# First sweep of a fused attention and feed-forward kernel: six held feed-forward units for each mixing step, and the last tokens' sums a slot later

## The chip, the core and the metric

The kernel runs on one core of one Trainium2 chip. The metric is device time in microseconds (us) of one execution. The engines are TensorE (PE, its weight loads PEld), VectorE (DVE), ScalarE (ACT), GpSimd (POOL) and SyncE (SP, which issues most transfers). Matrix results land in PSUM banks, from which VectorE and ScalarE fetch them. A bank can be written anew only when it has been fetched.

## The reference

```python
# B, H, S, D = 8, 8, 576, 64; d_model 512, rank 32, hidden 2048
scores = (1/sqrt(D)) * q @ k.T
cum = cumsum(log(clip(f, 1e-4, 1)))
scores = where(causal, -1e9, scores + cum[:, None] - cum[None, :])
attn = exp(scores - max(scores)); attn = attn / (sum(attn) + 1e-9)
x = (attn @ v), heads side by side            # (8, 576, 512)
u = x + ((x^T @ U) @ V)^T                     # mixing along the tokens, rank 32
out = u + relu(u @ w_ch1) @ w_ch2             # feed-forward
```

All in float32. The kernel splits each operand in a high and a low half and multiplies high by high, low by high and high by low, so one float32 product is three passes.

## The kernel before

The work is in two sweeps. The second (from about 740 us) does ten of the sixteen hidden chunks of the feed-forward part for all tokens and is not touched. The first does attention for 32 head pairs, four to a batch, and, beside it, the mixing and six of the sixteen hidden chunks.

**Steps and slots.** The function `step(t)` works on head pair t, and finishes pairs t-1 and t-2. A step has ten slots. In each slot TensorE gets, in this order: one score block (`score`, `score_tail`; lines L357, L358), transposes of the exponentials of the pair before (L453, in slots 0 to 2 and 6 to 8; of the last tokens, L467, in slot 5), in slots 0 and 7 a product with the values (L556), and in slots 3, 4 and 8 the turn of the result (L587), the small turn (L486, L488) and the projection on the rank (L622). After these comes what was left over for the step: a mixing unit, and a feed-forward unit (a filler). TensorE's order and the transfers' (SP) are as written; VectorE, ScalarE and GpSimd are ordered by a scheduler when the program is built. What follows a matmul on other engines is written into a list by `defer(phase, fn, slots)`, which hands it out that many slots later, lower phases first.

**Mixing steps.** When four pairs of batch b are done, the next step (t = 6, 10, 14, ..., 30) carries its ten mixing units, one to a slot: H0 to H4 in slots 0 to 4 (`hmix`, matmul L650, whose result VectorE adds to X at L651), Tu0 to Tu3 in slots 5 to 8 (`tu`, four transposes L664; ScalarE copies the high half, uh, L654; VectorE makes the low half, ul, L655), Tv in slot 9 (`tv`, L673).

**Feed-forward units.** Of each batch there are two groups of tokens. A unit A (`l1`, L713) is one hidden chunk; ScalarE takes the relu (hh, L721) and VectorE the low half (hl, L717). A unit B (`l2`, L731) is one of three parts of the output sum for 128 tokens; x names the block of tokens, and p0, p1, p2 the parts, which stay in one bank until the third is done. Then `use` adds X on VectorE (ost, L745) and SP stores it. For odd batches the second group has a third block, of the last 64 tokens of two batches (ci = 4); its `use` is the two adds L748 and L749. This block comes first of its group's B units.

**Banks.** H, Tu, Tv, A and B take banks of one pool, psF (tag F), which has two. Scores have two of their own (psS). A score's bank is free again when VectorE has taken its maximum (L378, L404) and ScalarE its exponential (L386, L414).

**What sets the order.** In a mixing step a held unit runs after the mixing unit in four slots:

```python
HELD = 4
...
if filler and (s in (0, 1, 3, 5) or ending):
    run_filler()
elif len(filler) > HELD and s in ROOM:
```

In the three steps between, the other units are spread over eight slots each (ROOM, all but 0 and 7) by a running credit, so that HELD remain. The held ones are the last B units of the batch: x0p2, x1p0, x1p1, x1p2. At the end of the sweep what is held goes beside the mixing of the last batch, where the second sweep's weights are decoded as well (`wb_unit`, VectorE lines L70 to L87).

Of the kernel before, what the change touches and what calls it, by code (L numbers as in the profile page):

```python
# [13 lines left out]
ALU = mybir.AluOpType  # L14
# [9 lines left out]
NM = 4  # L24
# [11 lines left out]
NX = 3  # L36
# [4 lines left out]
def tile_decay_attention_moe(ctx, tc, qk, v, f, U, V, w1, w2, out):  # L41
    nc = tc.nc
# [10 lines left out]
    def behind(ins, kind):  # L53
        tc.add_manual_dep(
            ins.ins, newest[kind].ins.name,
            mybir.DependencyInfo(mybir.DependencyClass.NoSync, mybir.DependencyReason.DATA), reason=f"order behind {kind}",
        )
# [80 lines left out]
    xn = [cst.tile([P, NM + 1, DM], F32, name=f"xn{i}") for i in range(NX)]  # L138
# [122 lines left out]
    filler = []  # L261
# [4 lines left out]
    def defer(phase, fn, slots=1):  # L266
        later.setdefault(now[0] + slots, []).append((phase, fn))
# [6 lines left out]
    def run_filler():  # L274
        w, fn = filler.pop(0)
        fn()
        return w
# [417 lines left out]
    def ffn_units(b):  # L695
        X = xn[b % NX]
        groups = ((0, 256), (256, 256)) if b % 2 == 0 else ((0, 256), (256, 384))
        units = []
        for t0, nt in groups:
            g = {}  # L700

            def l1(fc, t0=t0, nt=nt, g=g):
                uh, ul = cur
                if fc == 0:
                    g["hh"] = sf.tile([P, NA, 384], F32R, tag="hh", name=f"hh{b}_{t0}")
                    g["hl"] = sf.tile([P, NA, 384], F32R, tag="hl", name=f"hl{b}_{t0}")
                hh, hl = g["hh"], g["hl"]
                sl = slice(t0, t0 + nt)
                ps = psF.tile([P, 512], F32, tag="F", name=f"A{b}_{t0}_{fc}")
                m = 0  # L710
                for c in range(NDC):
                    for wt, ut in ((w1h, uh), (w1l, uh), (w1h, ul)):
                        nc.tensor.matmul(ps[:, :nt], wt[:, fc, c], ut[:, c, sl], start=m == 0, stop=m == 3 * NDC - 1)  # L713
                        m += 1

                def low():
                    nc.vector.scalar_tensor_tensor(  # L717
                        hl[:, fc, :nt], ps[:, :nt], 0.0, hh.bitcast(F32)[:, fc, :nt], op0=ALU.max, op1=ALU.subtract
                    )

                defer(3, lambda: nc.scalar.activation(hh[:, fc, :nt], ps[:, :nt], AF.Relu))  # L721
                defer(1, low, 2)

            def l2(x, part, t0=t0, g=g):
                hh, hl = g["hh"], g["hl"]
                if part == 0:
                    g["ps"] = psF.tile([P, 512], F32, tag="F", name=f"B{b}_{t0}_{x}")
                ps = g["ps"]
                for fc in range(2 * part, 2 * part + 2):
                    for m, (ht, wt) in enumerate(((hh, w2h), (hl, w2h), (hh, w2l))):  # L730
                        nc.tensor.matmul(  # L731
                            ps, ht[:, fc, P * x : P * x + P], wt[:, fc],
                            start=fc == 0 and m == 0, stop=fc == NA - 1 and m == 2,
                        )
                if part < NA // 2 - 1:
                    return
                ci = t0 // P + x

                def use():
                    if b == B - 1 and ci < NM:  # L740
                        nc.vector.tensor_tensor(X[:, ci], ps, X[:, ci], op=ALU.add)
                        return
                    ost = sf2.tile([P, DM], F32, tag="ost", name=f"ost{b}_{ci}")
                    if ci < NM:
                        nc.vector.tensor_tensor(ost, ps, X[:, ci], op=ALU.add)  # L745
                        nc.sync.dma_start(accd[b, ci], ost)
                    else:
                        nc.vector.tensor_tensor(ost[0:64], ps[0:64], X[0:64, NM], op=ALU.add)  # L748
                        nc.vector.tensor_tensor(ost[64:128], ps[64:128], xn[(b - 1) % NX][0:64, NM], op=ALU.add)  # L749
                        nc.sync.dma_start(accd[B, b // 2], ost)  # L750

                defer(1, use)

            units += [(12 * max(nt / 2400, 0.107), lambda fc=fc, l1=l1: l1(fc)) for fc in range(NA)]
            units += [
                (6 * 0.216, lambda x=x, part=part, l2=l2: l2(x, part)) for x in ((2, 0, 1) if nt > 2 * P else (0, 1)) for part in range(NA // 2)
            ]
        return units
# [1 line left out]
    NP = B * NHP  # L760
    SLOTS = 10
    ENGINES = (nc.scalar, nc.scalar, nc.gpsimd, nc.gpsimd, nc.gpsimd)
    HELD = 4
    with tc.manual_schedule(engines=None):
        fr, fl, cm0, dq = decay_log()
        nc.sync.dma_start(fr, f)
# [41 lines left out]
    def step(t):  # L808
# [3 lines left out]
        last, ending = t == LAST, t > LAST - 2  # L812
# [7 lines left out]
        for s in range(6 + 2 if last else SLOTS):  # L820
# [71 lines left out]
            if mixing:  # L892
                for _ in range(2 if t == MIX[0] else 1):
                    mixing.pop(0)[1]()
                if filler and (s in (0, 1, 3, 5) or ending):
                    run_filler()
            elif len(filler) > HELD and s in ROOM:

                ahead = sum(x >= s for x in ROOM) + len(ROOM) * (min(m for m in MIX if m > t) - 1 - t)
                credit[0] += (len(filler) - HELD) / max(ahead, 1)  # L900
                if credit[0] > 0.999 or t > LAST - 3:
                    credit[0] = max(credit[0] - 1, 0)
                    run_filler()
            if ps_ and s == 6:
                score(p, 1, 0)
            if px and s == (6 + 1 if last else 9) and st[c]["hp"] == NHP - 1:
                b = st[c]["b"]
                assert len(filler) <= HELD and not mixing
                mixing.extend(mix_units(b))
# [9 lines left out]
    with tc.manual_schedule(engines={ET.PE, ET.SP}):  # L919
        step(0)  # L920
    with tc.manual_schedule(engines={ET.PE}):
        for t in range(1, 7):
            step(t)
    with tc.manual_schedule(engines={ET.PE, ET.SP}):
        for t in range(7, LAST + 1):
            step(t)
        run_later()
# [585 lines left out]
```

## Time and profile before

| | |
|---|---|
| median of 3 runs | 1218.68 us (1218.43 to 1220.3) |
| the profiled execution | 1220.24 us |
| its span, first to last instruction | 1218.4 us |
| TensorE's granted clock | 1.000 |
| mixing step 10 (score of slot 0 to the next step's) | 181.06 to 201.79 |
| step 15 | 292.05 to 313.62 |

All durations below are of the profiled execution. A row in order of time has its start (us from the span's start), its length, engine, line, operation, tiles written and read (buffer numbers left out), sizes, count, and in brackets the idle time before it and what ended that. Matmuls overlap: the next can start before the modelled end of the last, so the distance between two starts tells more than the length. S is a score, St one of the last tokens, P and Ptl exponentials, T and T_v their transposes, PTh and PTl the two halves fetched from these, G the operands of the next scores, xh and xl the halves of the attention output.

### The profile page before, as it was taken

The numbers are of one execution on the slowest core, as the hardware profiler recorded it, in microseconds if no ns is written. First come the engines' busy times: TensorE is split into PE (matmuls) and PEld (weight loads), VectorE is DVE, ScalarE is ACT, GpSimd is POOL, SyncE is SP. The second block draws the span as 40 slices with busy tenths as digits, with TensorE's granted clock in tenths as the row PEclk, the third lists the DMA queues.
The fourth block names the chain that finished last, engine by engine and source line by source line (L and its number), as shares of the span: only waits on it lengthen the run. The fifth ranks groups of instructions, "written<-read, shape, count | busy, mean of one in ns | idle before, by whom it ended". The sixth has DMA issues, their size and how long they took to land.

```text
span 1218.4 us, 23835 instructions
## 1 busy us (share of the span) xinstructions
PE 1187.9 (97%) x8460; PEld 1084.7 (89%) x8460; DVE 931.2 (76%) x2249; ACT 738.6 (61%) x2027; POOL 523.9 (43%) x518
## 2 busy tenths in 40 slices
PE   8998999999999999999999999999999999999998
PEld 5887898988889988989989887788999999999998
DVE  8887878768778778787686798966777767778675
ACT  7777787767768758777676443434454544545443
POOL 4214554544545535454442000024575556555553
PEclk9999999999999999999999999999999999999999
DMA  5753335325235325425322357132514244243420
GB/s 155 194 140 122 102 87 167 102 78 168 75 88 167 90 79 150 119 70 177 81 85 83 110 175 216 54 104 70 156 53 139 89 137 123 91 134 92 134 53 36
DMA packets 81159, 138.47 MB, mean 114 GB/s; under 512 B 8752, under 2 KB 45616, under 8 KB 78992
## 3 DMA queue, kind: packets, MB, share of 16 engines
q1 hardware_dynamic: 79824, 128.56, 35.1%
q0 software_dynamic: 1152, 8.39, 3.7%
q8 instruction: 67, 1.10, 0.4%
q14 instruction: 52, 0.43, 0.1%
q10 hardware_dynamic: 64, 0.00, 0.0%
HBM read 101.08 MB, written 35.78 MB: 112 GB/s over the span
## 4 chain that ended last, share of the span: by engine, by line
PE 79%; DVE 10%; ACT 6%; issue 2%; DMA 2%; POOL 0%; SPq 0%; DVEq 0%; ACTq 0%; POOLq 0%
PE N L1156 12%; PE A L713 10%; PE A L1136 9%; PE B L731 9%; PE B L1136 7%; PE V L556 5%; PE T L453 4%; PE V L528 3%; PE S L357 3%; PE S L358 2%; PE B L1156 2%; PE S L354 2%; DMA sr<-in_w_dram 2%; PE O L1027 2%; PE O L1221 1%
## 5 line engine op out<-in xcount | busy, mean ns | idle before, releaser
L386 ACT ACTIVATE P<-S,nm 128x128 f32<-128x128 f32 (+3 forms) x256 | 137.5, 538 | 54.3 <-DVE nm L378 47.4
L197 POOL TENSOR_TENSOR hb<-xn,hb 128x256 fp32r<-128x256 f32 x136 | 113.6, 856 | 125.7 <-ACT hb L194 104.4
L378 DVE CUSTOM_DVE_ANT_0 S<-S,mask 128x128 f32<-128x128 f32 (+3 forms) x256 | 125.6, 496 | 53.4 <-PE S L358 46.5
L322 POOL CAST G<-qk 64x576 fp32r<-64x576 f32 x52 | 34.7, 667 | 248.9 <-PE St L358 148.2
L713 PE MATMUL A<-uh,w1h 128*128 128x256 f32 (+1 forms) x384 | 120.6, 314 | 1.9 <-DVE hl L717 1.9
L713 PE MATMUL A<-ul,w1h 128*128 128x256 f32 (+1 forms) x384 | 113.7, 296 | 0.0
L713 PE MATMUL A<-uh,w1l 128*128 128x256 f32 (+1 forms) x384 | 113.6, 296 | 0.0
L194 ACT CAST hb<-xn 128x256 fp32r<-128x256 f32 x136 | 51.8, 404 | 77.4 <-DVE xn L1142 42.9
L731 PE MATMUL B<-w2h,hh 128*128 128x512 f32 x216 | 90.5, 419 | 1.7 <-DVE ost L745 1.0
L453 PE MATMUL T<-ident,P 128*128 128x128 f32 x544 | 85.5, 273 | 0.0
L731 PE MATMUL B<-w2l,hh 128*128 128x512 f32 x216 | 85.1, 394 | 0.0
L731 PE MATMUL B<-w2h,hl 128*128 128x512 f32 x216 | 84.7, 392 | 0.0
L435 DVE TENSOR_TENSOR PTl<-T,PTh 128x512 fp32r<-128x512 f32 (+1 forms) x156 | 79.0, 524 | 6.6 <-ACT PTh L432 6.3
L1156 PE MATMUL N<-sw,hb 128*128 128x256 f32 x546 | 80.4, 283 | 0.1
L335 POOL TENSOR_TENSOR G<-qk,G 64x576 fp32r<-64x576 f32 x52 | 74.4, 1432 | 13.1 <-PE T L453 5.1
L1156 PE MATMUL N<-b2h,hb 128*128 128x256 f32 x420 | 79.9, 282 | 0.0
L336 POOL TENSOR_TENSOR G<-qk,G 64x576 fp32r<-64x576 f32 x52 | 75.3, 1449 | 4.9 <-ACT G L322 4.6
L713 PEld LDWEIGHTS A<-uh,w1h 128*128 128x128 f32 x384 | 72.9, 190 | 4.3 <-DVE hl L717 4.1
L357 PE MATMUL S<-G 128*128 128x128 f32 x208 | 70.3, 343 | 4.8 <-ACT P L386 3.1
L432 ACT CAST PTh<-T 128x512 fp32r<-128x512 f32 (+1 forms) x156 | 68.3, 469 | 10.1 <-PE T L453 9.6
L713 PEld LDWEIGHTS A<-uh,w1l 128*128 128x128 f32 x384 | 73.2, 191 | 0.3
L713 PEld LDWEIGHTS A<-ul,w1h 128*128 128x128 f32 x384 | 72.9, 190 | 0.0
(328 smaller groups left out, 3999.1 us busy)
## 6 DMA issues: line engine op xcount, KB each, us to landing
qk<-in_qk_dram SPq DMA_DIRECT2D x104, 288.0 KB
direct<-ud SPq DMA_DIRECT2D x48, 256.0 KB
sr<-in_w_dram SPq DMA_DIRECT2D x20, 512.0 KB
vr<-in_v_dram SPq DMA_DIRECT2D x32, 256.0 KB
accd<-ost SPq DMA_DIRECT2D x32, 256.0 KB
xn<-accd SPq DMA_DIRECT2D x8, 1024.0 KB
out_dram<-xn SPq DMA_DIRECT2D x32, 256.0 KB
ud<-uh SPq DMA_DIRECT2D x7, 1024.0 KB
```

The source lines that it names most:

```text
L197: leng.tensor_tensor(dl, src, dh.bitcast(F32), op=ALU.subtract)
L335: pin(el.tensor_tensor(g[oth, 2, cols], k[oth], gf[oth, 2, cols], op=ALU.subtract))
L336: pin(em.tensor_tensor(g[own, 1, cols], q[own], gf[own, 0, cols], op=ALU.subtract))
L357: nc.tensor.matmul(ps, G[j][:, 0, c0 : c0 + P], G[j][:, 2, cols], start=first, stop=False)
L378: newest["top"] = nc.vector.tensor_tensor_reduce(ps[:, :w], ps[:, :w], mask[:, 512 - w : 512], scale=-SCALE, scalar=3.0e38, op0=ALU.add, o ...
L386: nc.scalar.activation(pt, ps[:, :w], AF.Exp, bias=z["nm"][:, col : col + 1], scale=-1.0, accum_out=z["sm"][:, col : col + 1])
L435: defer(2, lambda: nc.vector.tensor_tensor(dstl, src, dsth.bitcast(F32), op=ALU.subtract))
L453: nc.tensor.transpose(tp[:, P * x : P * x + P], z["P"][j][i][:, P * c : P * c + P], ident)
L713: nc.tensor.matmul(ps[:, :nt], wt[:, fc, c], ut[:, c, sl], start=m == 0, stop=m == 3 * NDC - 1)
L731: nc.tensor.matmul(ps, ht[:, fc, P * x : P * x + P], wt[:, fc], start=fc == 0 and m == 0, stop=fc == NA - 1 and m == 2,)
L1136: nc.tensor.matmul(ps, a[x][:, c], b[y][:, c], start=start and m == 0, stop=m == 5, skip_group_check=not start)
L1156: nc.tensor.matmul(ps[:, y], a[p_][:, P * y : P * y + P], w[q_], start=start and y == 0 and m == 0, stop=stop and y == 1 and m == 2,)
```

## The change

Six units are held for a mixing step instead of four (x0p0, x0p1, x0p2, x1p0, x1p1, x1p2), and run in slots 0, 1, 2, 4, 5 and 7. The three steps between have two units fewer, so their units stand in other slots. The last tokens' adds are handed out two slots after their third part instead of one, and are put behind the newest maximum in VectorE's order (`behind`: a mark for the scheduler, no wait).

```diff
                     else:
-                        nc.vector.tensor_tensor(ost[0:64], ps[0:64], X[0:64, NM], op=ALU.add)
-                        nc.vector.tensor_tensor(ost[64:128], ps[64:128], xn[(b - 1) % NX][0:64, NM], op=ALU.add)
+                        behind(nc.vector.tensor_tensor(ost[0:64], ps[0:64], X[0:64, NM], op=ALU.add), "top")
+                        behind(nc.vector.tensor_tensor(ost[64:128], ps[64:128], xn[(b - 1) % NX][0:64, NM], op=ALU.add), "top")
                         nc.sync.dma_start(accd[B, b // 2], ost)
 
-                defer(1, use)
+                defer(1, use, 1 if ci < NM else 2)
...
-    HELD = 4
+    HELD = 6
...
-                if filler and (s in (0, 1, 3, 5) or ending):
+                if filler and (s in (0, 1, 2, 4, 5, 7) or ending):
```

Three places in the built order. First ScalarE in mixing step 10, slots 4 to 6 (L492 the small turn, L322 the next pair's operands, L606 xh, L654 the high half of Tu). Before:

```order
L492 CAST PT49_2385<-Ty9_8_2482 64x128
L322 CAST G0_91<-qk11_0_2364 128x576 x2
L432 CAST PTh9_2383<-T9_v_2435 128x2x2x64 x2
L606 CAST xh8_2492<-xn2_106 128x640
L654 CAST uh0_1310<-Tu1_0_2506 128x4x128
L414 ACTIVATE Ptl10_2523,sm10_2354<-St10_0_2477,nm10_2353 128x288
L414 ACTIVATE Ptl10_2523,sm10_2354<-St10_1_2497,nm10_2353 128x288
L432 CAST PTh9_2383<-T9_10_2537 128x512
L654 CAST uh0_1310<-Tu1_1_2542 128x4x128
```

and the same piece of ScalarE's order with the change:

```order
L492 CAST PT49_2371<-Ty9_8_2469 64x128
L606 CAST xh8_2486<-xn2_106 128x640
L322 CAST G0_91<-qk11_0_2350 128x576 x2
L432 CAST PTh9_2369<-T9_v_2419 128x2x2x64 x2
L414 ACTIVATE Ptl10_2514,sm10_2339<-St10_0_2464,nm10_2338 128x288
L414 ACTIVATE Ptl10_2514,sm10_2339<-St10_1_2491,nm10_2338 128x288
L654 CAST uh0_1310<-Tu1_0_2500 128x4x128
L432 CAST PTh9_2369<-T9_10_2528 128x512
L654 CAST uh0_1310<-Tu1_1_2533 128x4x128
```

The copy of Tu0 (L654, Tu1_0: batch 1, block 0) moved behind the two exponentials of the last tokens, and xh moved ahead of the operands.

Second, VectorE in the same step, slots 3 to 5, with the change (L589 the turned result, L504 the last rows of it, L496 the small turn's low half):

```order
L435 TENSOR_TENSOR PTl9_2370<-T9_v_2419,PTh9_2369 128x128
L745 TENSOR_TENSOR ost0_2_2434<-B0_256_0_2379,xn0_104 128x512
L378 ISA S10_03_2445,nm10_2338<-S10_03_2445,mask_93 128x512
L378 ISA nm10_2338 128x1
L589 TENSOR_TENSOR xn2_106<-Tx8_2448,rv8_2317 128x4x128
L651 TENSOR_TENSOR xn1_105<-H1_3_2453,xn1_105 128x512
L404 ISA St10_0_2464,nm10_2338<-St10_0_2464,mask_93 128x288
L404 ISA nm10_2338 128x1
L651 TENSOR_TENSOR xn1_105<-H1_4_2472,xn1_105 64x512
L496 TENSOR_TENSOR PT49_2371<-Ty9_8_2469,PT49_2371 64x128
L504 TENSOR_TENSOR xn2_106<-Ty9_8_2469,rv8_2317 64x128
```

Before, the row of L745 for this bank stood two slots earlier, and the rest in the same order; now the sum of block x0 stands at the head of this piece.

Third, VectorE around the last tokens' adds of batch 1. Before, in step 13, slot 7:

```order
L435 TENSOR_TENSOR PTl12_3279<-T12_10_3439,PTh12_3278 128x512
L748 TENSOR_TENSOR ost1_4_3455<-B1_256_2_3391,xn1_105 64x512
L749 TENSOR_TENSOR ost1_4_3455<-B1_256_2_3391,xn0_104 64x512
L378 ISA S13_10_3450,nm13_3246<-S13_10_3450,mask_93 128x128
L378 ISA nm13_3246 128x1
L378 ISA S13_11_3463,nm13_3246<-S13_11_3463,mask_93 128x256
```

and with the change, in mixing step 14, slot 1:

```order
L378 ISA S14_00_3536,nm14_3522<-S14_00_3536,mask_93 128x128
L378 ISA nm14_3522 128x1
L748 TENSOR_TENSOR ost1_4_3571<-B1_256_2_3431,xn1_105 64x512
L749 TENSOR_TENSOR ost1_4_3571<-B1_256_2_3431,xn0_104 64x512
L427 TENSOR_SCALAR sm13_3232<-sm13_3232 128x9
L428 RECIPROCAL rv13_3816<-sm13_3232 128x9
```

The adds moved from ahead of a maximum in step 13 to behind the first maximum of step 14.

On TensorE the units between mixing steps change slots. Slots 5 and 6 are where the prediction looks. Before, one of the two is empty in steps 15, 17, 23 and 25, and in 28, whose slot 6 holds an A unit of 384 tokens instead of 256. With the change one is empty in steps 7, 8, 11, 12, 13, 17, 20, 21, 25, 28 and 29; in 8, 12, 20 and 28 slot 6 is the empty one and slots 4 and 5 hold B units. At the end of the sweep two B units move from between the last small transposes and the last rank product to behind the first mixing units of batch 7.

## The prediction

> **What bounds the kernel now.** I began with the page's busy times, then took the waits of TensorE, then the first sweep by stretches of one step each, then single waits in order of time.
>
> ```profile
> PE 1187.9 (97%) x8460; PEld 1084.7 (89%) x8460; DVE 931.2 (76%) x2249; ACT 738.6 (61%) x2027; POOL 523.9 (43%) x518
> ```
>
> TensorE is the bound, and its matrix work does not change here. What the change can move is only the time in which TensorE waits. The table of waits (engine and line, waited for: us in total, times, longest) names the feed-forward banks:
>
> ```profile
> PE Tu L664 <- DVE ost L745: 2.1, 6, 0.3
> PE Tu L664 <- DVE ul L655: 1.0, 1, 1.0
> ```
>
> Six times means once in each mixing step that holds feed-forward units (steps 10, 14, 18, 22, 26, 30). A row of this table counts only idle time after the modelled end of a matmul, so below I take distances between starts. The table by stretches gives mixing step 10 (length, then busy time of PE, PEld, DVE, ACT, POOL, clock):
>
> ```profile
> 181.06:201.79 20.73, 20.06 (x135) 17.21 (x134) 17.99 (x48) 15.72 (x45) 10.05 (x9) 1.00 0.37 101
> ```
>
> Weights are loaded in 17.21 of 20.73 us and no engine is full: TensorE, VectorE and ScalarE wait for each other here. The clock is at 1.00, so no wait costs more than its own length. The step's second half in order of time, from the score of slot 3 on:
>
> ```profile
> 188.34 0.39 PE L357 MATMUL S<-G 128*128 128x512 f32 x1
> 189.28 0.51 PE L650 MATMUL H<-TS,VV 128*128 128x512 f32 x1
> 189.62 0.40 PE L731 MATMUL B<-w2h,hh 128*128 128x512 f32 x1
> 189.67 0.69 DVE L378 CUSTOM_DVE_ANT_0 S<-S,mask 128x512 f32<-128x512 f32 x1
> 190.28 0.69 DVE L589 TENSOR_TENSOR xn<-Tx,rv 128x512 f32<-128x512 f32 x1
> 190.88 0.68 DVE L651 TENSOR_TENSOR xn<-H,xn 128x512 f32<-128x512 f32 x1
> 191.02 0.29 PE L357 MATMUL St<-G 128*128 128x288 f32 x1
> 191.69 0.48 PE L650 MATMUL H<-TS,VV 128*64 128x512 f32 x1
> 191.86 0.47 DVE L404 CUSTOM_DVE_ANT_0 St<-St,mask 128x288 f32<-128x288 f32 x1 [0.29 <-PE St L358]
> 192.00 0.30 PE L357 MATMUL St<-G 128*128 128x288 f32 x1
> 192.38 1.25 ACT L322 CAST G<-qk 128x576 fp32r<-128x576 f32 x2 [0.16 <-PE St L357]
> 193.25 0.28 DVE L504 TENSOR_TENSOR xn<-Ty,rv 64x128 f32<-64x128 f32 x1
> 193.39 0.47 PE L731 MATMUL B<-w2h,hh 128*128 128x512 f32 x1
> 193.54 0.64 ACT L432 CAST PTh<-T_v 128x256 fp32r<-128x256 f32 x2
> 194.06 0.74 ACT L606 CAST xh<-xn 128x640 fp32r<-128x640 f32 x1
> 194.69 0.60 ACT L654 CAST uh<-Tu 128x512 fp32r<-128x512 f32 x1
> 194.85 0.60 PE L453 MATMUL T<-ident,P 128*128 128x128 f32 x4
> 195.05 0.69 DVE L745 TENSOR_TENSOR ost<-B,xn 128x512 f32<-128x512 f32 x1
> 195.17 0.52 ACT L414 ACTIVATE Ptl<-St,nm 128x288 f32<-128x288 f32 x1
> 195.66 0.68 DVE L655 TENSOR_TENSOR ul<-Tu,uh 128x512 fp32r<-128x512 f32 x1
> 195.80 0.66 PE L664 MATMUL Tu<-ident,xn 128*128 128x128 f32 x4 [0.35 <-DVE ost L745]
> 196.13 0.60 ACT L432 CAST PTh<-T 128x512 fp32r<-128x512 f32 x1
> ```
>
> The reader is to see the last wait: the second transpose group (Tu, slot 6) starts 0.95 behind T, whose four transposes take 0.44 (four steps of 0.11); 0.51 is lost until ost frees the bank. One feed-forward B unit is 194.85 - 193.39 = 1.46.
>
> **Part one, the mixing step.** Held B units (x is the block of 128 tokens, p the part) go from x0p2, x1p0, x1p1, x1p2 in slots 0, 1, 3, 5 to x0p0, x0p1, x0p2, x1p0, x1p1, x1p2 in slots 0, 1, 2, 4, 5, 7. The two more units, 2.92 us, come off the three steps before, so the work itself adds nothing in sum. Only waits count.
>
> Removed: in slot 1 the unit behind H waited for ost of the bank just finished; it now goes on in its own open bank.
>
> ```profile
> 185.28 0.47 PE L650 MATMUL H<-TS,VV 128*128 128x512 f32 x1
> 185.93 0.50 PE L731 MATMUL B<-w2h,hh 128*128 128x512 f32 x1 [0.17 <-DVE ost L745]
> 200.89 0.40 PE L358 MATMUL S<-G 128*128 128x512 f32 x1
> 201.43 0.43 PE L673 MATMUL Tv<-ident,xn 64*128 64x64 f32 x4
> ```
>
> H to B is 0.65 there against 0.34 at 189.28, so 0.31 goes. The wait at Tu (0.51) goes in its present form. Tv stands 0.54 behind a score matmul of 0.23 and gets a bank that ost has long freed: 0.31. Together -1.13.
>
> Added, first: the pool F has two banks. x0 holds one through slots 0 to 2, so H0 to H3 share the other; H4 takes x0's old bank, and x1p0 behind it must have the bank of H3. Let E be the start of the slot-3 score, right behind x0p2. VectorE's next work there is (order) ost, reduce, Tx, H3. ost starts 0.20 behind the next start on TensorE (195.05 - 194.85), then by pitch 0.61 (195.05 to 195.66), 0.61 (189.67 to 190.28), 0.60, and 0.68 for H3's add: it ends at E+2.70. TensorE reaches x1p0 at E + 1.28 (188.34 to 189.62) + 0.67 (191.02 to 191.69) + 0.31 = E+2.26. A wait of 0.5 with the hand-over; the next tail score (St1) then starts at E + 2.76 + 1.46 = E+4.22.
>
> Added, second and largest: x1 keeps its bank from slot 4 to slot 7, so Tu0 to Tu3 run through one bank, and Tu1 (slot 6) waits for Tu0's uh copy (ScalarE) and ul difference (VectorE). H3's add starts at E+2.02, St0's reduce 0.60 later, and from 191.86 to the end of L504 are 1.67: L504 ends at E+4.29. ScalarE's order then is xh, G twice, PTh twice, Ptl twice, uh: xh from E+4.34, 0.63 (194.06 to 194.69); G 1.16 (192.38 to 193.54); PTh 0.52 (to 194.06); Ptl 0.96 (195.17 to 196.13); so uh runs E+7.61 to E+8.21, ul to E+8.92, and Tu1 may start at E+8.98. TensorE is there at E + 4.22 + 2.85 (192.00 to 194.85) + 0.44 = E+7.51. The wait is 1.47; it is 1.1 if xh hides wholly. Tu2 and Tu3 come a values product and a B unit later, more cover than Tu1 has by a microsecond, and I give them no wait.
>
> Net per mixing step: 0.50 + 1.47 - 1.13 = +0.84; six times, +5.0. If neither new wait arose it would be -6.8; if xh, DVE and ACT each run 0.3 later, +8.6.
>
> The Trainium skill (Perfetto Trace Analysis, Optimizing Tensor Performance, Matmuls) says that independent matmul groups should rotate through different PSUM banks, so that evacuating one overlaps the next; four transpose groups in one bank are against it. By that rule Tu1 pays the whole evacuation less its cover, as in the sum; if it did not bind, a step would come to 0.50 - 1.13 and the term to -3.8. The row of the waits on ul (one of 1.0 us, in step 6, where transposes also come close behind each other) agrees.
>
> **Part two, the other steps.** Last tokens' sums. In steps 13, 21, 29 the two adds of L748 and L749 now stand ahead of the score's maximum:
>
> ```profile
> 264.29 0.67 DVE L748 TENSOR_TENSOR ost<-B,xn 64x512 f32<-64x512 f32 x1
> 264.98 0.69 DVE L749 TENSOR_TENSOR ost<-B,xn 64x512 f32<-64x512 f32 x1
> 265.61 0.31 PE L556 MATMUL V<-PTh,VS 128*128 128x320 f32 x1
> 266.65 0.44 PE L357 MATMUL S<-G 128*128 128x384 f32 x1 [0.73 <-ACT P L386]
> ```
>
> TensorE stands 1.04 behind a matmul of 0.15, so 0.89 goes, three times: -2.7. The adds now come after the maximum of the mixing step's slot 0 and have a values product, four transposes and H0 on TensorE as cover before x0p0 needs their bank, which I take to be enough for the 1.4 that they last. SP's store behind them moves a slot too; no load of that slot waits behind it.
>
> Empty slots. Two units fewer in three steps leave slot 5 or 6 empty more often. A step of before with slot 6 empty is step 15:
>
> ```profile
> 305.62 0.60 PE L453 MATMUL T<-ident,P 128*128 128x128 f32 x4
> 306.46 0.33 PE L357 MATMUL S<-G 128*128 128x128 f32 x1 [0.24 <-ACT Ptl L414]
> 306.94 0.39 PE L357 MATMUL S<-G 128*128 128x256 f32 x1
> ```
>
> 0.84 - 0.44 and 0.48 - 0.27 make 0.61 in which a score waits for a bank that the tail's exponentials free. Before, steps 15, 17, 23, 25 have it; by the order, 11, 13, 17, 21, 25, 29 will: +1.2, and 0.1 each for 8, 12, 20, 28, whose cover is a B unit without ScalarE work. Step 9's empty slot 1 costs what step 17's did. Step 7 loses one unit and, I take it, as much time, with half a microsecond of doubt either way. This part: -2.7 + 1.6 = -1.1, from -2.7 to +1.
>
> **Part three, the end of the sweep.** Two more units of batch 6 are left over. They stood between the last small transposes (Ty) and the last rank product (Tt):
>
> ```profile
> 685.34 0.69 DVE L608 TENSOR_TENSOR xl<-xn,xh 128x512 fp32r<-128x512 f32 x1
> 686.19 0.22 PE L622 MATMUL Tt<-xh,Us 128*64 128x128 f32 x1
> 690.00:710.00 20.00, 17.42 (x116) 15.05 (x115) 20.00 (x41) 8.66 (x18) 0.00 (x0) 1.00 0.57 186
> ```
>
> Tt waits for xl (end 686.03) with or without them, so the gap that they filled opens in full. But then VectorE decodes weights without a pause (20.00 of 20.00) and TensorE idles 2.6; the two units, 2.9, fall into that. I take 0; the bounds are -0.5 and +2.9.
>
> Sum: 5.0 - 1.1 + 0 = +3.9. The profiled execution took 1220.24, with a span of 1218.4 and 1.84 around it, 1.56 above the median of 1218.68. Span 1222.3; from the median, 1222.6.
>
> **Rivals.**
> *The mixing step only gains cover.* ScalarE has slack in sum (15.72 of 20.73). Were uh ahead of its queue, both new waits would vanish: -6.8 - 1.1, 1210.8. Against it stands the order, which puts uh behind six ScalarE instructions. The Trainium skill (Perfetto Trace Analysis, Optimization Strategy) advises interleaving regimes with different bounds, which is this case; the trace shows that the cover lies in slots 2, 4 and 7, not ahead of slot 6. Chance 0.08.
> *The waits swap evenly.* New waits of about 1.1 a step instead of 1.97, because an engine behind in one slot catches up during the next: 0 - 1.1, 1217.6. Speaks for it: 2.7 us of VectorE idle time in step 10. Chance 0.25.
> *Only the last tokens' sums count,* with no new score waits: -2.7, 1216.0. Chance 0.05.
> *The end of the sweep decides.* If VectorE's decodes wait for TensorE after Tt, the two units are not absorbed: +2.9 on top, 1225.5. It decides as soon as VectorE idles over 0.2 between 690 and 710. Chance 0.12.
>
> **Numbers.** The forecast has 0.50, its own range 1220.5 to 1225. 0.2% (2.4 us) is about what a measurement of this kernel can tell from no change. Slower: 0.42 of the forecast's 0.50 and the 0.12 of the sweep's end, 0.54. Same: 0.08 of the forecast and 0.22 of the even swap, 0.30. Faster: 0.08, 0.05 and 0.03 of the even swap, 0.16. The range 1216.0 to 1226.5 leaves out the first rival and the far bounds.
>
> **What would show it.** Right: the mixing steps last about 24.5 instead of 20.7, Tu waits for ul six times for 1.1 to 1.5 (start to start), B at L731 waits for xn of L651, and the wait at 266.65 is gone. Wrong: a mixing step of 23.5 or less, or Tu's waits under 0.5.

## The result, and the profile after

The changed kernel takes 1227.59 us (median of 6 runs, 1226.77 to 1229.89), the kernel before 1219.16 beside it (6 runs): ratio 1.007, with an interval of 1.006 to 1.0081. The forecast was 1222.6, and the measured time lies above its range (1216.0 to 1226.5). The profiled execution took 1227.23, with a span of 1225.4.

| piece of the span, us | before | after | difference |
|---|---|---|---|
| six mixing steps (10, 14, ..., 30) | 124.4 | 149.5 | +25.1 |
| eighteen steps between (7 to 29) | 392.8 | 375.0 | -17.8 |
| from step 31 to the end | 580.5 | 580.2 | -0.3 |
| span | 1218.4 | 1225.4 | +7.0 |

A B unit is six matmuls. Two of them in order of time, in the changed kernel:

```profile
279.43 0.39 PE L731 MATMUL B<-w2h,hh 128*128 128x512 f32 x1
279.66 0.39 PE L731 MATMUL B<-w2h,hl 128*128 128x512 f32 x1
```

Six pitches of 0.23 make 1.38, so the twelve moved units are 16.6 us of work that changed places. Without them the mixing steps lost 25.1 - 16.6 = 8.5 in waits, 1.42 each, where the forecast had 0.84 (at the forecast's own 1.46 for a unit it would be 1.27); the steps between gained 1.2, where it had 1.1. The other 1.4 us between the span's 7.0 and the medians' 8.4 are the profiled executions: that of before lies 1.1 above the median beside it, that of after 0.4 below its own.

The busy times, the table of TensorE's waits, and mixing step 14 in the table by stretches:

```profile
PE 1187.8 (97%) x8460; PEld 1085.2 (89%) x8460; DVE 933.1 (76%) x2249; ACT 738.7 (60%) x2027; POOL 526.7 (43%) x518
...
PE Tu L664 <- DVE ul L655: 11.2, 7, 1.7
PE B L731 <- DVE xn L651: 2.9, 6, 0.5
PE S L357 <- ACT Ptl L414: 2.0, 4, 0.9
...
271.88:296.80 24.92, 22.66 (x147) 19.43 (x146) 20.62 (x51) 15.13 (x43) 9.50 (x9) 1.00 0.34 95
```

The table of before had two rows for ost, the one that the prediction shows and this one:

```profile
PE B L731 <- DVE ost L745: 1.0, 6, 0.2
```

Both are gone, and the two waits that the prediction put in their place are there, once in each of the six steps: Tu for ul (its seventh is that of step 6, as before), B for H3's add. A mixing step takes 24.92 (24.5 was forecast). So the two waits are the forecast ones, and their size is not. Mixing step 14 from the score of slot 3 on, in order of time:

```profile
280.12 0.39 PE L357 MATMUL S<-G 128*128 128x512 f32 x1
281.91 0.47 PE L650 MATMUL H<-TS,VV 128*64 128x512 f32 x1
282.13 0.68 DVE L651 TENSOR_TENSOR xn<-H,xn 128x512 f32<-128x512 f32 x1
282.87 0.50 PE L731 MATMUL B<-w2h,hh 128*128 128x512 f32 x1 [0.48 <-DVE xn L651]
284.36 0.29 PE L357 MATMUL St<-G 128*128 128x288 f32 x1
287.16 0.60 PE L453 MATMUL T<-ident,P 128*128 128x128 f32 x4
287.28 0.51 ACT L414 ACTIVATE Ptl<-St,nm 128x288 f32<-128x288 f32 x1
287.38 1.40 POOL L336 TENSOR_TENSOR G<-qk,G 64x576 fp32r<-64x576 f32 x1
287.75 0.60 ACT L654 CAST uh<-Tu 128x512 fp32r<-128x512 f32 x1
287.91 0.89 DVE L426 TENSOR_TENSOR sm<-sm 128x1 f32<-128x1 f32 x1 [0.22 <-ACT Ptl L414]
288.72 0.68 DVE L655 TENSOR_TENSOR ul<-Tu,uh 128x512 fp32r<-128x512 f32 x1
289.46 0.66 PE L664 MATMUL Tu<-ident,xn 128*128 128x128 f32 x4 [1.70 <-DVE ul L655]
```

With E = 280.12 the forecast's chain can be laid beside it. H3's add ends at E+2.69 (2.70 forecast), St1 starts at E+4.24 (4.22), uh at E+7.63 (7.61). Then it parts: uh ends at 288.35, but ul starts at 288.72, behind L426, an add of one column of 128 numbers (the sum of the tail's exponentials) that holds VectorE for 0.81. Tu1 starts at E+9.34 instead of E+8.98; its wait is 289.46 - 287.16 - 0.44 = 1.86 instead of 1.47. And TensorE comes to H4 0.16 earlier than reckoned, so B waits 282.87 - 281.91 - 0.31 = 0.65 instead of 0.50. The two make 2.51. The rest of the sum is seen from start to start, step 14 beside step 10 of before (181.06, 188.34, 192.00, 195.80, 201.79 there; 271.88, 280.12, 284.36, 289.46, 296.80 here), with 1.38 taken off for each of the two units:

| stretch of the mixing step, us | forecast | measured |
|---|---|---|
| start to E (the wait for ost in slot 1 goes) | -0.31 | -0.42 |
| E to St1 (B for H3's add) | +0.50 | +0.58 |
| St1 to Tu1 (1.47 new, 0.51 gone) | +0.96 | +1.30 |
| Tu1 to the end (Tv) | -0.31 | -0.03 |
| sum | +0.84 | +1.43 |

So the last line was missed by nearly as much as the Tu1 line. Tv does start earlier, 0.33 behind the second product of its score (295.94) instead of 0.54, but the next step's score does not follow it sooner. That score takes the bank of slot 8's score, and it starts 0.81 behind that one's exponential (L386); before it was 0.84. The end of the step in the changed kernel, and two rows of before:

```profile
295.99 0.58 ACT L386 ACTIVATE P<-S,nm 128x384 f32<-128x384 f32 x1
296.27 0.46 PE L673 MATMUL Tv<-ident,xn 64*128 64x64 f32 x4
296.80 0.30 PE L357 MATMUL S<-G 128*128 128x128 f32 x1
```

```profile
200.95 0.58 ACT L386 ACTIVATE P<-S,nm 128x384 f32<-128x384 f32 x1
201.79 0.33 PE L357 MATMUL S<-G 128*128 128x128 f32 x1
```

Why the add L426 takes so long, one row of the groups by line tells (name, count, then ns least, median and most, first and last start), that of L426 in the changed kernel:

```profile
L426 DVE TENSOR_TENSOR sm<-sm x32: 143/510/989, 18.1 to 659.3; 128x1 f32<-128x1 f32 x32
```

The same instruction takes 0.14 or 0.99. In the rows above it ends at 288.80, and GpSimd's subtraction L336 at 288.78. Of the 32 instances of L426, 24 start while a subtraction of L335 or L336 runs on GpSimd, and every one of these ends 0.015 to 0.021 us behind it; the other eight take 0.14 to 0.16, one of them beside a GpSimd memset. The Trainium skill (SBUF — State Buffer, Who interferes with whom) says that a VectorE instruction with both inputs in SBUF contends with a GpSimd instruction that reads SBUF, and that the later of the two is blocked until the first has finished. The trace agrees, to 0.02 us.

### The profile page after: what moved, and what is told of

It reads as the page before. It is cut to its first block, busy times and chain, and to the rows that moved or that the text cites. A ratio compares the mean times of both kernels' runs of the same rounds, so it can differ in the third digit from the quotient of the medians.

```text
span 1225.4 us, 23859 instructions
## 1 busy us (share of the span) xinstructions
PE 1187.8 (97%) x8460; PEld 1085.2 (89%) x8460; DVE 933.1 (76%) x2249; ACT 738.7 (60%) x2027; POOL 526.7 (43%) x518
## 4 chain that ended last, share of the span: by engine, by line
PE 84%; DVE 8%; ACT 5%; issue 1%; DMA 1%; SPq 0%; DVEq 0%; ACTq 0%
PE N L1156 12%; PE B L731 10%; PE A L713 10%; PE A L1136 9%; PE B L1136 7%; PE V L556 5%; PE T L453 4%; PE V L528 3%; PE S L357 3%; PE S L358 2%; PE O L1027 2%; PE Hb L1006 2%; PE B L1156 2%; PE S L354 2%; ACT G L322 2%
## 5 line engine op out<-in xcount | busy, mean ns | idle before, releaser
L386 ACT ACTIVATE P<-S,nm 128x128 f32<-128x128 f32 (+3 forms) x256 | 137.2, 537 | 53.4 <-DVE nm L378 44.9
L322 POOL CAST G<-qk 64x576 fp32r<-64x576 f32 x52 | 34.7, 667 | 228.1 <-PE St L358 129.2
L335 POOL TENSOR_TENSOR G<-qk,G 64x576 fp32r<-64x576 f32 x52 | 74.8, 1439 | 13.1 <-PE T L453 5.1
L336 POOL TENSOR_TENSOR G<-qk,G 64x576 fp32r<-64x576 f32 x52 | 74.7, 1436 | 8.7 <-ACT G L322 8.3
```

The lines of the kernel that those rows point to most:

```text
L335: pin(el.tensor_tensor(g[oth, 2, cols], k[oth], gf[oth, 2, cols], op=ALU.subtract))
L336: pin(em.tensor_tensor(g[own, 1, cols], q[own], gf[own, 0, cols], op=ALU.subtract))
L386: nc.scalar.activation(pt, ps[:, :w], AF.Exp, bias=z["nm"][:, col : col + 1], scale=-1.0, accum_out=z["sm"][:, col : col + 1])
```

## The experiments

Theory A: the loss is the two waits of the mixing step, x1's bank held open over Tu0 to Tu2 and H0 to H3 in one bank. Against it: the moved adds (rival), the other steps, or the end of the sweep (rival D).

### The two halves of the change alone

The adds moved as in the change, four units in the old slots (e1_sums_only):

```diff
-    HELD = 6
+    HELD = 4
...
-                if filler and (s in (0, 1, 2, 4, 5, 7) or ending):
+                if filler and (s in (0, 1, 3, 5) or ending):
```

> The last tokens' adds moved as in the change, four units held in the old slots. Theory A (the waits in the six mixing steps belong to the six held units, and the moved adds are a gain by themselves): steps 13, 21 and 29 are about 0.85 us shorter than before, mixing steps 20.7 as before, and the time is 2.6 us below that of before, ratio 0.998. Rival (the moved adds delay the mixing step behind them, by the bank that they free later): steps 13, 21, 29 shorter, but mixing steps 14, 22 and 30 longer by as much or more, ratio 1.000 or above.

Measured: 1217.23 (11 runs; before 1219.02, ratio 0.9987, 0.9978 to 0.9995). Mixing steps stay at 20.7. Steps 13, 21 and 29 are 0.46 to 0.48 shorter, not 0.85: the score's wait of 0.89 is gone, but the adds now stand ahead of a PTl whose bank the rank product needs, and that waits instead (TensorE, step 13):

```profile
267.58 0.27 PE L622 MATMUL Tt<-xh,Us 128*64 128x128 f32 x1 [0.32 <-DVE PTl L435]
```

So about half of the forecast's -2.7 was there to be had: 1.4. The other half, six units without the adds' move (e2_held6_only):

```diff
-                        behind(nc.vector.tensor_tensor(ost[0:64], ps[0:64], X[0:64, NM], op=ALU.add), "top")
-                        behind(nc.vector.tensor_tensor(ost[64:128], ps[64:128], xn[(b - 1) % NX][0:64, NM], op=ALU.add), "top")
+                        nc.vector.tensor_tensor(ost[0:64], ps[0:64], X[0:64, NM], op=ALU.add)
+                        nc.vector.tensor_tensor(ost[64:128], ps[64:128], xn[(b - 1) % NX][0:64, NM], op=ALU.add)
...
-                defer(1, use, 1 if ci < NM else 2)
+                defer(1, use)
```

> Six units held in slots 0, 1, 2, 4, 5, 7, the last tokens' adds where they were before. Theory A: mixing steps at 24.9 as with the whole change, steps 13, 21, 29 longer than with it by 0.85 each, so 2.6 us above the changed kernel, about 1230. Rival (moved adds are part of the loss): mixing steps 14, 22, 30 shorter than 24.9 by 0.5 or more, and the time at or below the changed kernel's 1227.6.

Measured: 1228.21 (4 runs; 1.0079, 1.0065 to 1.0093), and every step from 8 to 30 as long as with the whole change, to 0.04. Steps 13, 21 and 29 take 23.41 with and without the adds' move. With six units held the third part of that block falls so late in step 13 that its adds run at 271.94, in the mixing step, anyway. Neither expectation held: the move gives nothing here and costs nothing. So the whole loss comes with the six units.

### Other slots for the same units

x1 shut before Tu1 (e3_slots_0_to_5):

```diff
-                if filler and (s in (0, 1, 2, 4, 5, 7) or ending):
+                if filler and (s in (0, 1, 2, 3, 4, 5) or ending):
```

> The changed kernel with the six units in slots 0 to 5: block x1 closes its bank in slot 5, before Tu1, and takes it in slot 3, behind x0's sum. Theory A (x1's open bank makes H4's successor wait 0.64 for H3's add, and Tu1 1.86 for Tu0's copy and difference): both waits go, Tu1 waits about 0.5 for ost as it did before the change, a mixing step takes about 22.9 instead of 24.9, and the time falls by 12 us to about 1215.5, below the kernel before. Rival (a mixing step with six units is held up by VectorE and ScalarE, whatever the slot): mixing steps of 24.3 or more and a time within 4 us of the changed kernel.

Measured: 1220.71 (11 runs; 1.0014, 1.0005 to 1.0023), and 1220.26 as e11_slots_again. A mixing step takes 23.17, 1.75 less (2.0 expected): B waits for nothing, Tu1 for ost, 0.86. Theory A holds for the mixing step. But of the 12 us only 7 came: from step 31 to the end it is 584.3 instead of 580.2. There the table by stretches shows what the kernel before does not have (the granted clock is the figure ahead of the last two):

```profile
679.50:682.91 3.41, 1.65 (x13) 1.24 (x11) 2.14 (x5) 1.11 (x2) 0.00 (x0) 1.00 0.00 0
682.91:689.74 6.83, 5.72 (x19) 4.61 (x20) 4.63 (x11) 2.35 (x5) 0.00 (x0) 0.50 0.00 0
```

The two units between Ty and Tt are missing, so TensorE is busy for 1.65 of 3.41 us there. Then its clock is halved for 6.83 us, and the B units go at a pitch of 0.43 instead of 0.23:

```profile
686.14 0.63 PE L731 MATMUL B<-w2h,hl 128*128 128x512 f32 x1
686.57 0.63 PE L731 MATMUL B<-w2l,hh 128*128 128x512 f32 x1
```

The changed kernel has the same hole (2.13 of 5 us busy from 690.24), but its profiled execution kept the clock at 1.00. Of the eight profiled executions with the hole six show the drop, four for 6.83 us and two for 3.41; of the nine whose hole is filled, none at this place.

### The end of the sweep

Four units left over for the last batch that mixes inside the sweep, in the changed kernel (e5_end_undone) and with the slots 0 to 5 (e6_slots_0_to_5_end):

```diff
-            elif len(filler) > HELD and s in ROOM:
+            elif len(filler) > (HELD if t < MIX[-2] else 4) and s in ROOM:
...
-                credit[0] += (len(filler) - HELD) / max(ahead, 1)
+                credit[0] += (len(filler) - (HELD if t < MIX[-2] else 4)) / max(ahead, 1)
```

> The changed kernel, but the last batch that mixes inside the sweep leaves four units over as before the change, so the two units stand between Ty and Tt again. Theory A (the mixing steps alone make the loss, the end of the sweep costs nothing): the gap before Tt is filled, the steps up to 31 are as with the change, and the time stays within 1 us of 1227.6. Rival D (the hole of 2.9 us before Tt lets TensorE's granted clock fall to 0.5 to 0.8 for some 5 us in many executions, as the trace of e3_slots_0_to_5 has it between 680 and 690): clock at 1.00 throughout the end of the sweep, and the time 1.5 to 2.5 us lower, about 1225.5.

> Units in slots 0 to 5, and four units left over at the end of the sweep as before the change. Theory A: as e3_slots_0_to_5, mixing steps 23.2, step 31 starts 2.7 us earlier than before the change, and the time stays at e3's 1220.7 if the hole costs nothing. Rival D (the hole lets the clock fall): the 2.7 us arrive at the end, about 1216.5, ratio 0.998 to the kernel before.

Measured: e5 1226.66 (5 runs; 1.0059, 1.0046 to 1.0073), 0.9 below the changed kernel, with overlapping intervals; e6 **1214.73** (5 runs; 0.9965, 0.9953 to 0.9978), 6 below e3, with intervals far apart. e6 beats both kernels. Its mixing step, and what is left to wait for there:

```profile
180.07:203.24 23.17, 22.37 (x147) 19.57 (x146) 18.38 (x50) 16.11 (x44) 9.67 (x9) 1.00 0.33 90
...
PE Tu L664 <- DVE ost L745: 4.2, 6, 0.7
```

To part the clock from the missing work, ten matmuls on zeros were put into the hole, whose result nothing uses: on e3 (e9_busy_gap) and on the changed kernel (e12_changed_busy_gap), beside e3 once more.

```diff
             if px and s == (6 if last else 8):
+                if last:
+                    stream(psT.tile([P, 512], F32, tag="T", name="fill"), 10)
                 ranks(c)
```

> The kernel of e3_slots_0_to_5 with ten matmuls on zeros (128x128 by 128x512, 0.22 us each) into a spare bank between Ty and Tt at the end of the sweep, where the two units are missing; they compute nothing that is used, and Tt's second product waits for xl there anyway. Clock theory (the loss of e3 behind the hole is the granted clock, 0.77 and 0.55 in two stretches of 5 us): the clock stays at 1.00, the work behind Tt goes at full pace, and the time is 3 to 4 us below that of e11_slots_again, about 1217. Rival (the two units are missing there as work, they come later in a place where they aren't hidden): the clock stays up but the time stays within 1 us of e11.

> The kernel of e3_slots_0_to_5 unchanged, on the same chip as e9 and e12. Clock theory: again about 1220.7, and a granted clock under 0.9 behind the hole if this execution has the fall. Rival (the 6 us between e3 and e6 were the chip or the hour): below 1219.

> The changed kernel itself with the same ten matmuls on zeros between Ty and Tt. Clock theory: the clock stays at 1.00 and the time is about 1 us below the changed kernel's 1227.6, as for e5_end_undone (1226.7), the rest of the loss being in the mixing steps. Rival (the hole costs the changed kernel nothing, and 1.0 us of e5 is the two units as work): no change, 1227.6.

Measured on one chip: e9 1217.46 (11 runs; 0.9988, 0.9979 to 0.9996) against e11's 1220.26 (11 runs; 1.0009, 1.0 to 1.0018). The clock stays up:

```profile
679.59:684.59 5.00, 4.02 (x26) 2.51 (x26) 2.14 (x6) 2.49 (x6) 0.00 (x0) 1.00 0.00 0
684.59:689.59 5.00, 5.00 (x28) 4.12 (x27) 5.00 (x11) 1.53 (x3) 0.00 (x0) 1.00 0.00 0
```

2.8 us come back without any useful work being moved: that part is the clock. The other 2.3, between e9 and e10_no_sums (below, on the same chip, with the units themselves in the hole), are the two units as work, so here both theories were half right. In the changed kernel the filled hole gives 1226.55 (5 runs; 1.0063, 1.005 to 1.0076), 1.0 less than 1227.59, as the filled end of e5; single intervals overlap, so neither pair alone shows that this 1.0 is real. Taken together, nine of the ten executions of the changed kernel with the end filled lie below 1227.2, and ten of the eleven without (e16, below, included) above it.

With the slots of e3 the two units cost 2.3 as work, with those of the change next to nothing. The traces show where the pairs part. Behind step 31's first score the last matmul of a B unit starts at 108.0 with zeros in the hole (e9) and at 105.6 with the units (e10); in the changed kernel it is 107.9 (e12) and 106.4 (e5). So the missing units cost 1.5 to 2.4 in both. Behind that, at the start of the second sweep, TensorE waits for VectorE's hb (L998) for 1.2 in e9, 0.8 in e10 and 0.6 in e5, and not at all in e12. Why that wait differs stays open.

The Trainium skill (TensorE: Matmul & The Clock Gate, What's actually happening) says that the array goes to half its clock after an idle window of some 3.4 us, and that the window runs freely and isn't started by the kernel. The trace agrees on the half (0.50, pitch 0.43 against 0.23) and on a window that runs by itself: within each execution the clock changes lie a whole number of 3.413 us apart, in e3 at 682.91, 689.74 and 1218.81 (the end of the span), 2 and 155 windows.

On that grid the traces also show why some executions escape, and that the window need not be idle throughout. In the window ahead of the six drops TensorE is busy for 0.97 to 1.65 of 3.41 us (1.65 in e3, above); in the two executions without a drop the emptiest window has 1.88 (e7) and, in the changed kernel, whose grid is counted back from its clock change at 1225.32, this:

```profile
689.42:692.84 3.42, 1.77 (x14) 1.37 (x12) 2.14 (x6) 1.11 (x2) 0.00 (x0) 1.00 0.00 0
```

The same hole is shared between two windows there. The line lies near half a window in these eight; it is not a rule, since e10 has a drop of 3.41 in the first sweep (from 104.97) behind a window with 2.04.

Does e6 need the moved adds? The same kernel without them (e10_no_sums, edit as in e2):

> The kernel of e6_slots_0_to_5_end with the last tokens' adds where they were before the change. If what e2_held6_only showed (with six units held, steps 13, 21 and 29 have no wait for the adds to remove) holds in this order too: steps 13, 21, 29 at 23.4 and the time within 0.5 us of e6's 1214.7. Rival (the adds need their move here, since the mixing step behind them is tighter): 1.5 to 2.6 us more.

Measured: 1215.18 (6 runs; 0.9967, 0.9956 to 0.9979), the same as e6.

### Five units, x1 shut a slot earlier

```diff
-    HELD = 6
+    HELD = 5
...
-                if filler and (s in (0, 1, 2, 4, 5, 7) or ending):
+                if filler and (s in (0, 1, 2, 3, 4) or ending):
```

with the end as in e5 (e8_held5_slots_0_to_4).

> Five units held (x0p1, x0p2, x1p0, x1p1, x1p2) in slots 0 to 4, four left over at the end of the sweep. Theory A (a Tu waits where the other bank is still open or its sum not yet taken): x1's sum has a whole slot before Tu1 needs its bank, so Tu1 waits under 0.2, x1p0 in slot 2 behind x0's sum 0.3; a mixing step takes about 21.7 (20.73 before, 1.39 more work, 0.5 less wait), the three steps between lose a unit, and the time is 4 us below the kernel before, about 1215. Rival (VectorE is behind in slots 4 to 6 whatever the bank, so the wait reappears at Tu2 or at a score): a mixing step of 22.1 or more, no gain over the kernel with only the sums moved, 1217.2.

Measured: 1225.26 (5 runs; 1.0045, 1.0033 to 1.0058), a mixing step of 22.6 to 22.8. The rival was right: Tu1 waits for nothing, TensorE is ready for the score of slot 7 at 286.86, and that waits 0.9 for the bank that ScalarE's exponentials hold (step 14):

```profile
287.12 0.51 ACT L414 ACTIVATE Ptl<-St,nm 128x288 f32<-128x288 f32 x1
287.77 0.33 PE L357 MATMUL S<-G 128*128 128x128 f32 x1 [0.75 <-ACT Ptl L414]
```

The three steps between pay too: 20.4 in step 16 instead of 18.7 with six units; over all eighteen it is 387.6 instead of 374.8 in e6, of which the six units that stand there again are 8.3. The bank of ost was not the last thing to end there.

### What the missed 0.37 is

L426 put behind Tu0's low half (e4_sum_behind_ul), then behind Tu3's (e7_sum_behind_last_ul, the same edit with "ul3"), then given to GpSimd (e13_sum_on_gpsimd), beside the changed kernel once more:

```diff
-        nc.vector.tensor_tensor(sm[:, 8:9], sm[:, 8:9], sm[:, 9:10], op=ALU.add)
+        first = nc.vector.tensor_tensor(sm[:, 8:9], sm[:, 8:9], sm[:, 9:10], op=ALU.add)
+        if p in MIX:
+            behind(first, "ul0")
...
-            defer(1, lambda: nc.vector.tensor_tensor(dl, src, dh.bitcast(F32), op=ALU.subtract), 2)
+            def low():
+                newest["ul%s" % i] = nc.vector.tensor_tensor(dl, src, dh.bitcast(F32), op=ALU.subtract)
+
+            defer(1, low, 2)
...
```

```diff
-        nc.vector.tensor_tensor(sm[:, 8:9], sm[:, 8:9], sm[:, 9:10], op=ALU.add)
+        (nc.gpsimd if p in MIX else nc.vector).tensor_tensor(sm[:, 8:9], sm[:, 8:9], sm[:, 9:10], op=ALU.add)
```

> The changed kernel, with the sum of the tail's exponentials (L426 on VectorE) of the mixing step's pair put behind the low half of Tu0 (ul, L655) in VectorE's order; nothing else differs. Theory A (the wait at Tu1 is the whole chain of Tu0's evacuation, and L426 stands in it with 0.37): Tu1's start-to-start excess falls from 1.86 to about 1.5, a mixing step from 24.92 to 24.55, the time by 2.2 us to about 1225.4. Rival (ScalarE's queue and the bank hand-over make up the wait, L426 only fills a gap): no change, 1227.6.

Measured: 1228.62 (4 runs; 1.0081, 1.0067 to 1.0094), a mixing step of 24.96: no gain. Both theories were short. Tu1's wait fell to 1.53 as expected, and Tu2 got a new one of 0.34, because the add, now beside GpSimd's L335, holds up Tu1's low half instead (the edit shifts lines: L658 is ul here, L669 Tu):

```profile
288.88 1.40 POOL L335 TENSOR_TENSOR G<-qk,G 64x576 fp32r<-64x576 f32 x1
289.02 1.28 DVE L426 TENSOR_TENSOR sm<-sm 128x1 f32<-128x1 f32 x1
289.16 0.66 PE L669 MATMUL Tu<-ident,xn 128*128 128x128 f32 x4 [1.37 <-DVE ul L658]
291.42 0.68 DVE L658 TENSOR_TENSOR ul<-Tu,uh 128x512 fp32r<-128x512 f32 x1
292.25 0.41 PE L669 MATMUL Tu<-ident,xn 128*128 128x128 f32 x2 [0.18 <-DVE ul L658]
```

> The changed kernel, with the sum of the tail's exponentials (L426 and the operations behind it, about 1.3 us of VectorE) behind the low half of Tu3 instead of Tu0. Theory A2 (Tu1's and Tu2's waits are the queue of VectorE between Tu0's and Tu1's low halves; behind Tu0's the sum only handed 0.35 from Tu1's wait to Tu2's): Tu1 waits 1.53 as in e4_sum_behind_ul and Tu2 no longer, a mixing step takes 24.55, the time is 2.2 us below the changed kernel. Rival (another engine sets Tu2, ScalarE's copy or the values product): Tu2 still waits 0.3 and a mixing step stays at 24.9.

> The changed kernel with the sum of the tail's exponentials (L426) of the mixing step's pair done by GpSimd, behind its subtraction of L335, instead of VectorE; the same number. Port theory (the 128x1 add on VectorE lasts 0.15 alone, but when it starts beside a GpSimd subtraction it ends with that, here 0.66 late, and the low half of Tu0 stands behind it): ul starts right behind uh, Tu1's excess falls from 1.86 to about 1.5, no wait at Tu2 as in e7_sum_behind_last_ul, and no loss in the next step as e7 had; a mixing step takes 24.57 instead of 24.92, the time is 2.1 us below e16_changed_again. Rival (another operation of VectorE takes the time, or the next step loses it as in e7): within 1 us of e16.

> The changed kernel itself, on the same chip as e13. About 1227.6, ratio 1.007 to the kernel before; the granted clock behind the hole before Tt falls in some executions and not in others.

Measured: e7 1230.31 (4 runs; 1.0091, 1.0077 to 1.0105); e13 1231.34 (4 runs; 1.0099, 1.0085 to 1.0113); e16 1228.09 (5 runs; 1.0073, 1.0059 to 1.0087). In both, mixing steps take 24.6 (24.57 was expected), Tu1 waits 1.53 and Tu2 no longer: the 0.33 to 0.37 a step is that add. But the step behind each mixing step is 0.8 longer (20.25 instead of 19.46 in step 15), more than was won. There the next operation on the same tile, L427, starts 0.04 behind a GpSimd subtraction instead of 0.03 ahead of it. First three rows of e13, then the same place in the changed kernel:

```profile
300.04 1.43 POOL L335 TENSOR_TENSOR G<-qk,G 64x576 fp32r<-64x576 f32 x1
300.08 1.42 DVE L427 TENSOR_SCALAR sm<-sm 128x9 f32<-128x9 f32 x1 [0.33 <-ACT P L386]
303.24 0.52 PE L453 MATMUL T_v<-ident,P 128*128 128x128 f32 x3 [0.59 <-DVE xT L576]
```

```profile
299.26 0.17 DVE L427 TENSOR_SCALAR sm<-sm 128x9 f32<-128x9 f32 x1 [0.25 <-ACT P L386]
299.29 1.44 POOL L335 TENSOR_TENSOR G<-qk,G 64x576 fp32r<-64x576 f32 x1
```

0.17 or 1.42 for 128 x 9 numbers, decided by 0.07 us. The same edit on e6, for the sums of all pairs from 7 on (`p > NF`; e15_best_sums_on_gpsimd):

> The kernel of e6_slots_0_to_5_end with the sum of L426 on GpSimd in all steps. Port theory: VectorE is free 0.3 to 0.9 us earlier once a step, but in this order no wait of TensorE stands behind that sum in a mixing step (Tu1 waits for ost, which comes ahead of it): mixing steps stay at 23.2, the score waits of slot 7 in the steps between may lose 0.2, so the time is 0 to 2 us below e6's 1214.7. Rival (GpSimd's operands for the next scores come later behind the sum): above 1215.5.

Measured: 1219.72 (11 runs; 1.0005, 0.9996 to 1.0013), 5 above e6. Mixing steps stay at 23.2 as expected; the steps behind them (11, 15, 19, 23, 27) are 0.8 longer each, with L427 at 1.42, and from step 31 on it is 2.0 more.

## Why the prediction missed

*What bounds the kernel, and the mechanism:* right for the two new waits. No other wait grew by more than 0.2 in a mixing step, and e3 and e6, which shut x1's bank before Tu1, took them away.

*Part one, the net wait of a mixing step (+0.84):* this step failed, by its size, in two of its terms. The first is Tu1's wait. "uh runs E+7.61 to E+8.21, ul to E+8.92" was right up to uh; it let ul start where uh ends. VectorE's built order has a row between, which I did not look for, because before the change it stands behind ul:

```
before:                        after:
L745 ost1_3 <- B1_256_1        L435 PTl13 <- T13_v
L655 ul2 <- Tu2_0              L426 sm14 <- sm14
L426 sm14 <- sm14              L655 ul2 <- Tu2_0
```

So ul starts 0.37 late, and the line from St1 to Tu1 comes out 0.34 above the forecast, of the 0.59 between +0.84 and +1.43. The second is Tv: "gets a bank that ost has long freed: 0.31" was right of Tv and wrong of the step, since the score behind Tv waits for an exponential in both kernels. Of 0.31 only 0.03 came, so 0.28 was missed. The other two lines nearly cancel: +0.08 with B's wait, since TensorE comes to H4 earlier, and -0.11 up to E. Over the six steps it is +8.5 instead of +5.0. The part's upper bound, +8.6, held, but the range over all parts ended at 1226.5, +7.8 from the median, and the medians moved by 8.4. To see the row would not have been enough. The trace of before has it in the same slot of step 10:

```profile
196.29 0.32 DVE L426 TENSOR_TENSOR sm<-sm 128x1 f32<-128x1 f32 x1
196.66 0.30 DVE L378 CUSTOM_DVE_ANT_0 S<-S,mask 128x128 f32<-128x128 f32 x1
```

At that pitch of 0.37, and ready when the second Ptl has given its sum (287.88 in step 14), it would end before uh does (287.91 + 0.37 = 288.28 against 288.35) and delay nothing. That it holds VectorE for 0.81 comes from GpSimd's row beside it.

*Part two (-1.1):* right in sum (-1.2), wrong in its terms. The adds' move is worth 1.4 alone, not 2.7, as the stall goes on to Tt, and nothing with six units, where the slots of step 13 do the same. By groups of three steps, each without 2.76 for its two units, the forecast was about +0.1, +0.4, -0.6, -0.2, -0.6 and -0.2 (7 to 9 first, 27 to 29 last), and +1.7, +0.3, -2.0, -0.2, -0.7 and -0.3 were measured. That the sum came out is luck: the first group lost what the third gained.

*Part three (0):* near in the profiled executions (-0.3), by luck, and short by about 1 in the medians, if e5 and e12 are taken at their word. I priced the hole as idle time that VectorE's decodes absorb. Most of it was not absorbed: the last matmul of a B unit starts 108.4 behind step 31's first score, 106.3 before, so 2.1 of the two units' 2.9 stayed. From there to the end the changed kernel takes 2.4 less (471.8 instead of 474.2). Of this 1.6 is a wait at the start of the second sweep that the profiled execution of before has and that of the changed kernel has not (e5 and e10, with the units in the hole as before, have 0.6 and 0.8):

```profile
PE O L1027 <- DVE hb L998: 1.6, 3, 0.8
```

"The clock is at 1.00, so no wait costs more than its own length" failed here too. That the hole can halve the clock for the work behind it was not among the rivals; the rival on the end of the sweep had the place and not the mechanism.

*Rivals:* the even swap (1217.6) fell, since the waits are larger than the forecast ones and not smaller. That only the last tokens' sums count (1216.0) is e1's 1217.2 without the six units. That the mixing step only gains cover is nearest to e6: not by uh coming earlier, but by shutting the bank.

## What to carry to other kernels

When a copy or a subtraction that frees a bank is timed from the rows of another order, read every row that the new order puts between its inputs and itself on its own engine, however small, and look at what GpSimd runs beside it. Count a wait as gone only when the next matmul behind it can start earlier too. Place a group that stays open over several slots so that it shuts before other work has to rotate through the banks; it was worth 1.75 us in each of six steps here. And work that is moved away from a place where TensorE waits for others takes the clock's cover with it: the price of a hole is the wait and, in six of eight executions here, 3.4 or 6.8 us of half pace behind it.

## What the runs showed of the hardware

A VectorE add of 128 x 1 in SBUF takes 0.14 to 0.18 alone and up to 1.32 (e4) beside a GpSimd subtraction of 64x576, ending 0.02 behind it; a 128x9 tensor_scalar 0.15 to 0.18 alone and up to 1.43, ending 0.03 behind it. The reciprocal of the same nine columns (L428) takes 0.20 to 0.22 in either company, and a PTl that reads its first input from a bank takes 0.67 beside L335, as elsewhere. TensorE's clock fell to 0.50 for 3.41 or 6.83 us in the six of eight profiled executions whose hole left it busy for at most 1.65 of a window of 3.41, and stayed at 1.00 in the two with 1.77 and 1.88; ten matmuls on zeros in the hole kept it up. The clock changes of one execution lie whole multiples of 3.413 us apart.
